# Attention in groups of three key blocks: another order for the evacuation, for GpSimd's preparation, for the adds and for a weight decode

## The chip, the cores and the metric

The kernel runs on one core of a Trainium2 chip. Five engines work side by side, each on a list of its own in the order in which the program issues it: TensorE (PE, with its weight loads PEld), VectorE (DVE), ScalarE (ACT), GpSimd (POOL) and SyncE (SP), which here only issues DMA transfers. An instruction that waits holds up everything behind it on its engine. The metric is the time of one execution on the device in microseconds.

## The reference, cut to what matters

Attention over pooled queries, then two mixture and gating stages on its output. The change touches the attention alone; 16 heads are worked on as 8 pairs.

```python
q_pool = q.reshape(B, H, S // 2, 2, D).mean(axis=3)            # B 2, H 8, S 1152, D 64
scores = scale * np.matmul(q_pool, k.transpose(0, 1, 3, 2))
scores = scores - np.max(scores, axis=-1, keepdims=True)
attn = np.exp(scores)
attn = attn / (np.sum(attn, axis=-1, keepdims=True) + 1e-09)
x = np.matmul(attn, v)
...
x = _moe_ref(x, ...)       # routing to 8 experts by argmax
x = _moe2_ref(x, w_in, w_out)
```

## The kernel before, in words

**Steps.** A pair of heads `p` has 9 blocks of 128 keys; one block is a step `t`, and `g = 9p + t` counts steps through all 8 pairs. In each step the loop at L655 to L679 issues, in this order: `scores(p, t)` (eight products and three exponentials into a tile `Pt`); the functions of slot 0; the early ("pre") maximum products; the functions of slot 1; in every third step the products of three finished blocks with v (`pv`, 24 products); in step 0 the evacuation `evac_x` of the finished pair; in step 6 `max_rows`; then `psums`, the row sums of the three blocks by products with a small matrix; in step 0 `evac_s`; the functions of slot 2; the late ("post") maximum products; the functions of slot 3. `at_step(p, t, f, slot=k)` puts a function into a slot. The last pair works in groups of two blocks.

**Exact products.** Queries and keys are split into a rounded part and a rest. `qhi`, `khi` (ScalarE) write the rounded parts `QS` and `At`, `qlo` (VectorE) and `klo` (GpSimd, tile `Bt`) the rests, `qcopy` (GpSimd) copies a half of `QS` to `qb`. They work one or two pairs ahead: in the loop `n = p + 1` and `m = p + 2`. `load_k`, `load_q`, `load_v` and `load_raw` issue the transfers; a key tile `kd` has two buffers, so `load_k` waits until `khi`, `klo` and `kdiff` of an earlier one are done.

**Maxima.** The row maximum of a unit (128 queries of a head; 9 units in a pair) comes from three products over 384 keys (`max_chunk`, c = 0, 1, 2), c = 1 against the key difference `KD` (tile `kx`, made by `kdiff` on GpSimd). ScalarE applies Relu to c = 1 and writes it to SBUF, VectorE reduces c = 0 and merges c = 2 with that. `step_chunks` deals them out to the steps, one pair ahead or two. Three PSUM buffers `mx` serve them. `max_cols` and `max_rows` turn the maxima into two rows of `qb`.

**Sums.** For three blocks VectorE adds the first two (`add_tile`, tile `st`), and `psums` takes that sum and the third. `psums` writes the same PSUM banks that `evac_x` reads.

**Weights.** The weights of the last stage arrive as 64-bit numbers and are decoded in the shadow of the attention: 23 tiles here. `raw_ahead` loads up to two tiles ahead, `decode_step` does one half of a tile (VectorE), `decode_abs` the absolute values (ScalarE) that the second half needs. `decode` calls `decode_abs` itself where it has not run yet.

## Time and profile of the kernel before

| what | us |
|---|---|
| median of three runs | 717.72 (716.46 to 718.08) |
| the profiled execution | 715.45 |
| its span, first to last instruction | 713.3 |
| first scores of pair 0 | 21.87 |
| first row sums of pair 1, step 0 | 67.88 |
| the same of pair 7 | 281.86 |
| last row sums | 314.74 |

Over the span TensorE is busy 90%, VectorE 69%, ScalarE 55%, GpSimd 30%. The attention is the stretch from 21.87 to about 317 us. In the rows below a line number is that of the kernel before; L91, L94, L97 and L100 are helpers that many functions share, so there the names of the tiles tell what an instruction is: `wd<-pv` on ACT is `evac_x`, `sm<-pv` `evac_s`, `wd<-mx` Relu, `dm` the absolute values and the decode, `st<-pt` the add, `kx<-kd` `kdiff`, `Bt<-kd,at` `klo`, `qb<-qs` `qcopy`, `qs<-tq` `qhi` on ACT and `qlo` on DVE. L324 are the products with v, L349 those of the row sums, L307 to L316 the scores. A bracket tells how long the engine had been idle before the instruction, and what ended that.

### The profile page before, as it was taken

To read this page: it belongs to the slowest core of one execution; us is meant where nothing else is said; L and a number is where in the kernel's file an instruction comes from. 1 tells how busy PE (TensorE), PEld (TensorE's weight loads), DVE (VectorE), ACT (ScalarE), POOL (GpSimd) and SP (SyncE) were. 2 spreads that over 40 slices of the span, in tenths; PEclk is the share of its full clock that TensorE was granted. 3 is DMA by queue.
4 is the path that set the end of the run, shared out by engine and by line. 5 is a ranking of instruction groups with operands and counts; after the bars stand their busy time and mean duration, and the time that the engine had idled before them with its cause. 6 is when DMAs were issued, how large, how long until landed. Compare 5 with 4: busy or idle time off the path is not lost. (4 is left out here: it accounts for less than half of the span.)

```text
span 713.3 us, 11655 instructions
## 1 busy us (share of the span) xinstructions
PE 644.0 (90%) x4319; PEld 510.2 (72%) x4319; DVE 490.4 (69%) x1010; ACT 391.9 (55%) x811; POOL 211.1 (30%) x195
## 2 busy tenths in 40 slices
PE   4798999997979999876998999997899999999997
PEld 3566766765757676545886886966788899999895
DVE  5667867674746764775745697611999977897875
ACT  7766776765655665522425546532666554555543
POOL 7443342423313120003503323410322232232322
PEclk9989999999998999998998999999999999999999
DMA  6674535352533112307839978682000020001001
GB/s 225 224 213 122 158 106 141 107 164 79 150 91 96 50 64 78 119 19 235 332 137 330 356 257 309 238 292 74 0 1 0 1 91 1 0 1 45 1 0 44
DMA packets 26641, 88.33 MB, mean 124 GB/s; under 512 B 2886, under 2 KB 7631, under 8 KB 22482
## 3 DMA queue, kind: packets, MB, share of 16 engines
q1 hardware_dynamic: 21264, 73.23, 29.3%
q0 software_dynamic: 3568, 8.79, 5.3%
q10 hardware_dynamic: 1746, 5.51, 2.2%
q8 instruction: 35, 0.57, 0.3%
q14 instruction: 28, 0.23, 0.1%
HBM read 79.65 MB, written 8.39 MB: 123 GB/s over the span
## 5 line engine op out<-in xcount | busy, mean ns | idle before, releaser
L91 ACT ACTIVATE pt<-sc 128x320 f32<-128x320 f32 (+1 forms) x216 | 96.5, 489 | 24.7 <-PE sc L309 23.3
L100 POOL TENSOR_SCALAR u<-u 128x384 f32<-128x384 f32 x48 | 60.2, 1255 | 152.1 <-ACT u L91 122.9
L324 PE MATMUL pv<-pt,vt 128*64 128x288 f32 x576 | 78.9, 424 | 0.0
L94 POOL TENSOR_TENSOR Bt<-kd,at 64x576 fp32r<-64x576 f32 x32 | 54.7, 1729 | 64.3 <-PE sc L310 59.1
L915 PE MATMUL zps<-yh,wh 128*128 128x384 f32 x188 | 64.3, 342 | 1.7 <-DVE n L97 1.7
L324 PEld LDWEIGHTS pv<-pt,vt 128*64 128x64 f32 x576 | 40.5, 142 | 32.9 <-issue 10.8
L917 PE MATMUL zps<-yl,wh 128*128 128x384 f32 x188 | 63.3, 337 | 0.0
L916 PE MATMUL zps<-yh,wd 128*128 128x384 f32 x180 | 61.0, 339 | 0.0
L1355 PE MATMUL ops<-wh,gl 128*128 128x512 f32 x144 | 57.7, 403 | 3.0 <-DVE gl L94 2.5
L103 DVE TENSOR_REDUCE Mp<-mx 128x1 f32<-128x384 f32 x72 | 39.9, 554 | 29.6 <-PE mx L230 29.4
L1355 PE MATMUL ops<-wh,gh 128*128 128x512 f32 x144 | 56.8, 395 | 0.2 <-ACT gh L91 0.2
L1355 PE MATMUL ops<-wd,gh 128*128 128x512 f32 x135 | 53.1, 394 | 0.0
L230 PE MATMUL mx<-at,qs 128*128 128x384 f32 x120 | 38.1, 388 | 12.4 <-DVE qs L94 7.7
L91 ACT ACTIVATE l<-n,two 128x384 f32<-128x384 f32 x48 | 29.5, 615 | 25.0 <-DVE n L97 25.0
L94 DVE TENSOR_TENSOR st<-pt 128x1152 f32<-128x1152 f32 x25 | 39.1, 1566 | 5.2 <-ACT pt L91 5.1
L91 ACT ACTIVATE wd<-mx 128x384 f32<-128x384 f32 x63 | 29.1, 498 | 22.7 <-PE mx L230 11.7
L91 ACT ACTIVATE u<-zps 128x384 f32<-128x384 f32 x48 | 23.2, 483 | 33.1 <-PE zps L917 30.0
L97 DVE SCALAR_TENSOR_TENSOR l<-n,r 128x384 f32<-128x384 f32 x48 | 26.6, 554 | 19.4 <-ACT r L91 19.4
L915 PEld LDWEIGHTS zps<-yh,wh 128*128 128x128 f32 x188 | 35.6, 189 | 3.6 <-ACT r L91 2.0
L244 DVE CUSTOM_DVE_ANT_0 wd<-mx,wd 128x384 f32<-128x384 f32 x63 | 34.5, 549 | 4.3 <-PE mx L230 2.9
L1355 PEld LDWEIGHTS ops<-wh,gl 128*128 128x128 f32 x144 | 27.0, 188 | 14.0 <-DVE gl L94 7.1
L91 ACT ACTIVATE gh<-n 128x384 fp32r<-128x384 f32 x48 | 24.8, 517 | 20.6 <-DVE n L97 20.4
(297 smaller groups left out, 1702.0 us busy)
## 6 DMA issues: line engine op xcount, KB each, us to landing
wt<-in_w SPq DMA_DIRECT2D x32, 1024.0 KB, 5.6
kd<-in_kt SPq DMA_DIRECT2D x16, 576.0 KB, 3.8
wraw<-in_wio SPq DMA_DIRECT2D x12, 512.0 KB, 4.0
wd<-in_wio SPq DMA_DIRECT2D x11, 512.0 KB, 4.5
vt<-in_v SPq DMA_DIRECT2D x8, 576.0 KB, 5.1
wraw<-in_wio ACTq DMA_DIRECT2D x9, 512.0 KB, 6.1
tq<-in_qt SPq DMA_DIRECT2D x12, 288.0 KB, 5.9
tq<-in_qt POOLq DMA_DIRECT2D x12, 288.0 KB, 5.2
```

Of the source, the lines that this page charges most:

```text
L91: A.activation(out=out, in_=in_, func=func, **kw)
L94: eng.tensor_tensor(out=out, in0=a, in1=b, op=op)
L97: V.scalar_tensor_tensor(out=out, in0=a, scalar=s, in1=b, op0=op0, op1=op1)
L100: eng.tensor_scalar(out=out, in0=a, scalar1=s1, scalar2=s2, op0=op0, op1=op1)
L103: V.tensor_reduce(out=out, in_=in_, axis=AX.X, op=op)
L230: mm(ps, lhsT=QS[p, h][:, j * P:(j + 1) * P], rhs=keys(h), start=True, stop=True)
L244: V.tensor_tensor_reduce(out=r_, in0=ps, in1=r_, scale=1.0, scalar=-3.0e38, op0=ALU.add, op1=ALU.max, accum_out=Mp[p % 2][:, h, j, 1:2])
L324: mm(pvt[p][64 * h:64 * h + 64, f, :HQ], lhsT=vt[p][:, t, h, :], rhs=Pt[p, t][:, h, f * HQ:(f + 1) * HQ], start=t == 0, stop=t == KT - 1, ...
L915: mm(out_, lhsT=a, rhs=c, start=first, stop=False)
L916: mm(out_, lhsT=b_, rhs=c, start=False, stop=False)
L917: mm(out_, lhsT=a, rhs=d, start=False, stop=last_)
L1355: mm(opt[b_, j], lhsT=(g_, g_, gl_)[i], rhs=(wo, wl_, wo)[i], start=f == 0 and i == 0, stop=f == NF - 1 and i == 2)
```

## The change

- `psums` is issued ahead of `evac_x`, in step 0 of each pair and at the end.
- `add_tile` runs in the step of its group (0, 3 and 6), behind the pre products, in place of the step before (2, 5, 8).
- GpSimd's `klo`, `qcopy` and `kdiff` of the pairs ahead go to slot 3 of steps 0, 3 and 6, and each lot but pair 0's starts with `after(n, u)`, a copy of one column on GpSimd that reads the maximum of unit `u`, c = 0, and so waits for it.
- `qhi`, `khi`, `qlo` of pair m move between steps; `khi(m, 1)` goes to step 0 of the next pair, so `at` needs 5 buffers and not 6. `load_k` and `load_q` go one step later.
- `decode_abs` ahead of need runs only for loads that are at least three steps old; `raw_ahead` runs behind the halves; pairs 1 to 6 take 5 halves each (before 5 and 4 in turn), the last pair correspondingly fewer.
- In pair 0 the products c = 1 run one step ahead, those of the first two units ahead of its first scores in place of two filler products. `x_tr`, `x_out` move behind the post products.

```diff
--- before.py
+++ after.py
@@ -175,7 +175,7 @@
         SP.dma_start(out=vt[p], in_=v[p])
 
     DEC_M = 32
-    DEC_A, DEC_L = 23, [2, 2, 1, 2, 2, 1, 2, 2, 1]
+    DEC_A, DEC_L = 23, [2, 1, 2, 1, 2, 1, 2, 1, 2]
     tqt = {}
 
     def qsum(p, h):
@@ -194,8 +194,13 @@
     def qmix(p, h):
         act(QM[p % 2][:, 192 * h:192 * h + 64], QS[p, h][:, 4 * P:].bitcast(F32))
 
+    def qb_(p, h):
+        if (p, h) not in QB:
+            QB[p, h] = ap.tile([P, SQ], F32R, name="qb", bufs=NBL)
+        return QB[p, h]
+
     def qcopy(p, h):
-        QB[p, h] = ap.tile([P, SQ], F32R, name="qb", bufs=NBL)
+        qb_(p, h)
         if p:
             G.tensor_copy(QB[p, h][:64], QS[p, h][:64].bitcast(F32))
         else:
@@ -203,7 +208,7 @@
 
     def khi(p, h, c):
         if c == 0:
-            At[p, h] = ap.tile([P, S], F32R, name="at", bufs=NB)
+            At[p, h] = ap.tile([P, S], F32R, name="at", bufs=NB - 1)
         cs_ = slice(c * SQ, (c + 1) * SQ)
         act(At[p, h][:, cs_], kd[p, h][:, cs_])
 
@@ -256,13 +261,12 @@
 
     units = [(h, j) for h in range(2) for j in range(4)] + [(0, 4)]
     chunks = ahead(units)
-    FIRST = [[0, 1], [2], [3], [4, 5], [6, 7], [8]]
+    FIRST = [[0, 1], [2], [3], [4, 5], [6, 7], [8], []]
 
     def step_chunks(p, t):
 
         if p == 0 and t < 6:
-            us = FIRST[t]
-            return [(1, *units[u], c) for c in (1, 0) for u in us], [(1, *units[u], 2) for u in us]
+            return [(1, *units[u], c) for u in FIRST[t] for c in (0, 2)], [(1, *units[u], 1) for u in FIRST[t + 1]]
         n, u = (p + 1, t + 3) if t < 6 else (p + 2, t - 6)
         if n >= NPAIR:
             return [], []
@@ -289,7 +293,7 @@
         ps1 = mxp.tile([P, 512], F32, name="mx")
         T.transpose(ps1[:34, :P], mt[:, 4, :], ident)
         for h in range(2):
-            qb = QB[p, h]
+            qb = qb_(p, h)
             act(qb[64:66, :512], ps0[32 * h:32 * h + 2, :])
             act(qb[64:66, 512:], ps1[:2, 64 * h:64 * h + 64])
 
@@ -334,9 +338,11 @@
         g = 9 * p + t
         return [divmod(i, KT) for i in range(g - 3, g)] if t % 3 == 0 and g else []
 
-    def add_tile(p, t):
-        St[p] = ap.tile([P, 2, SQ], F32, name="st", bufs=1)
-        tt(V, St[p], Pt[p, t - 2], Pt[p, t - 1], ALU.add)
+    def add_tile(tiles):
+        p = tiles[0][0]
+        if len(tiles) > 1:
+            St[p] = ap.tile([P, 2, SQ], F32, name="st", bufs=1)
+            tt(V, St[p], Pt[tiles[0]], Pt[tiles[1]], ALU.add)
 
     def psums(tiles):
         p = tiles[0][0]
@@ -467,9 +473,10 @@
         (SP if pool is ap else A).dma_start(out=wraw[i].rearrange("p a b -> p (a b)"), in_=wio[f, :, 512 * c:512 * (c + 1)].bitcast(I32))
 
     def decode_abs(pool, i=None):
-        if i is None:
+        early = i is None
+        if early:
             i = dec[0] + (dec[0] in dmt)
-        if i not in dmt and i in wraw:
+        if i not in dmt and i in wraw and now[0] - since.get(i, 0) >= (3 if early else 0):
             m = dmt[i] = pool.tile([P, 512], F32, name="dm", bufs=2)
             act(m, wraw[i][:, :, 1].bitcast(F32), AF.Abs)
 
@@ -504,66 +511,68 @@
     at_step(-1, 7, lambda: qhi(1, 0))
     at_step(-1, 8, lambda: max_cols(0), lambda: (qlo(1, 0), qmix(1, 0)))
     at_step(0, 0, lambda: (khi(1, 0, 1), klo(1, 0, 0), klo(1, 0, 1), load_k(2, 0), load_q(2, 0)))
-    at_step(0, 1, lambda: (qsum(1, 1), qhi(1, 1), khi(1, 1, 0), khi(1, 1, 1), kdiff(1, 1), qlo(1, 1), qmix(1, 1)), slot=1)
-    at_step(0, 2, lambda: (klo(1, 1, 0), klo(1, 1, 1), qcopy(1, 0), load_k(2, 1), load_q(2, 1)), slot=1)
-    at_step(0, 3, lambda: (qhi(2, 0), khi(2, 0, 0)), slot=1)
-    at_step(0, 4, lambda: (khi(2, 0, 1), kdiff(2, 0), qlo(2, 0)), slot=1)
-    at_step(0, 5, lambda: qcopy(1, 1), slot=1)
-    at_step(0, 6, lambda: (qhi(2, 1), khi(2, 1, 0), khi(2, 1, 1), kdiff(2, 1)), slot=1)
-    at_step(0, 7, lambda: qlo(2, 1), slot=1)
+    at_step(0, 1, lambda: (qsum(1, 1), qhi(1, 1), khi(1, 1, 0), kdiff(1, 1), qlo(1, 1)), slot=1)
+    at_step(0, 2, lambda: khi(1, 1, 1))
+    at_step(0, 3, lambda: qmix(1, 1), slot=1)
+    at_step(0, 2, lambda: (klo(1, 1, 0), klo(1, 1, 1), load_k(2, 1), load_q(2, 1)), slot=1)
+    at_step(0, 3, lambda: (qhi(2, 0), qlo(2, 0)), slot=1)
+    at_step(0, 4, lambda: (kdiff(2, 0), qcopy(1, 0)), slot=1)
+    at_step(0, 6, lambda: (khi(2, 0, 0), khi(2, 0, 1), qhi(2, 1), qlo(2, 1)), slot=1)
+    at_step(0, 6, lambda: (qcopy(1, 1), kdiff(2, 1)), slot=3)
     at_step(-1, 8, lambda: load_v(0))
+    wait_ = ap.tile([P, 1], F32, name="wait")
+
+    def after(n, u):
+        if n < NPAIR:
+            h, j = units[u]
+            G.tensor_copy(wait_, Mp[n % 2][:, h, j, 0:1])
+
+    def piece(k):
+        return [lambda: decode_step(ap, DEC_A)] * k + [lambda: raw_ahead(ap, DEC_A)]
+
+    def abs_():
+        return lambda: decode_abs(ap)
+
     for p in range(NPAIR):
         n, m = p + 1, p + 2
         if n < NPAIR:
             at_step(p, 4, lambda n=n: load_v(n), slot=1)
             at_step(p, 6, lambda n=n: max_cols(n))
             if p:
-                at_step(p, 0, lambda n=n: (klo(n, 0, 0), klo(n, 0, 1)))
-                at_step(p, 1, lambda n=n: (klo(n, 1, 0), klo(n, 1, 1)))
-                at_step(p, 3, lambda n=n: qcopy(n, 0), slot=2)
-                at_step(p, 5, lambda n=n: qcopy(n, 1), slot=1)
+                at_step(p, 0, lambda n=n: (after(n, 3), klo(n, 0, 0), klo(n, 0, 1), klo(n, 1, 0)), slot=3)
+                at_step(p, 3, lambda n=n: (after(n, 6), klo(n, 1, 1), qcopy(n, 0)), slot=3)
+                at_step(p, 6, lambda n=n: (after(n + 1, 0), qcopy(n, 1)), slot=3)
         if m < NPAIR:
             if p:
-                at_step(p, 0, lambda m=m: (qhi(m, 0), qhi(m, 1)), slot=1)
-                at_step(p, 1, lambda m=m: load_k(m, 0), slot=1)
-                at_step(p, 3, lambda m=m: (kdiff(m, 0), khi(m, 0, 0), khi(m, 0, 1), qlo(m, 0), qlo(m, 1), load_k(m, 1)), slot=1)
-                at_step(p, 6, lambda m=m: (khi(m, 1, 0), khi(m, 1, 1), kdiff(m, 1)), slot=1)
+                at_step(p, 2, lambda m=m: load_k(m, 0), slot=1)
+                at_step(p, 3, lambda m=m: (qhi(m, 0), qhi(m, 1), qlo(m, 0)), slot=1)
+                at_step(p, 3, lambda m=m: kdiff(m, 0), slot=3)
+                at_step(p, 4, lambda m=m: load_k(m, 1), slot=1)
+                at_step(p, 6, lambda m=m: (khi(m, 0, 0), khi(m, 0, 1), qlo(m, 1)), slot=1)
+                at_step(p, 6, lambda m=m: kdiff(m, 1), slot=3)
+            at_step(p + 1, 0, lambda m=m: (khi(m, 1, 0), khi(m, 1, 1)), slot=1)
             at_step(p + 1, 0, lambda m=m: (qmix(m, 0), qmix(m, 1)), slot=3)
         if p + 3 < NPAIR:
-            at_step(p, 6, lambda p=p: (load_q(p + 3, 0), load_q(p + 3, 1)), slot=2)
+            at_step(p, 7, lambda p=p: (load_q(p + 3, 0), load_q(p + 3, 1)), slot=1)
         if p:
             at_step(p, 4 if p == last else 3, lambda p=p: sum_log(p - 1), slot=1)
             at_step(p, 6, lambda p=p: (sum_tr(p - 1), sum_rec(p - 1)), slot=1)
-            at_step(p, 6, lambda p=p: [(x_tr(p - 1, i), x_out(p - 1, i)) for i in range(2)], slot=2)
+            at_step(p, 6, lambda p=p: [(x_tr(p - 1, i), x_out(p - 1, i)) for i in range(2)], slot=3)
             if p < last:
                 at_step(p, 8, lambda p=p: x_put(p - 1), slot=1)
-        if p < last:
-            for t in (2, 5, 8):
-                at_step(p, t, lambda p=p, t=t: add_tile(p, t))
-        else:
-            for t in (2, 4, 6, 8):
-                at_step(p, t, lambda p=p, t=t: add_tile(p, t))
-
-        def piece(k):
-            return [lambda: (raw_ahead(ap, DEC_A), decode_step(ap, DEC_A))] * k
-
-        def ahead_(k=1):
-            return [lambda: (raw_ahead(ap, DEC_A), decode_abs(ap))]
-
         if p == last:
             for t in range(9):
-                at_step(p, t, *piece(DEC_L[t]), *ahead_(), slot=1)
+                at_step(p, t, *piece(DEC_L[t]), slot=1)
+                at_step(p, t, abs_(), slot=3)
         else:
             if p == 0:
                 at_step(0, 0, lambda: raw_ahead(ap, DEC_A), slot=3)
             else:
-                at_step(p, 0, *piece(2), *ahead_(), slot=1)
-            at_step(p, 3, *piece(2), *ahead_(), slot=1)
-            if p == 0:
-                at_step(p, 6, *piece(2), slot=1)
-            elif p % 2:
-                at_step(p, 6, *piece(1), slot=1)
-            at_step(p, 6, *ahead_(), slot=2)
+                at_step(p, 0, *piece(2), slot=1)
+                at_step(p, 3, *piece(2), slot=1)
+            at_step(p, 3, abs_(), slot=2)
+            at_step(p, 6, *piece(2 if p == 0 else 1), slot=1)
+            at_step(p, 6, abs_(), slot=2)
 
     A.preload_act_table_set("natural_log_exp_and_others")
     load_q(0, 0)
@@ -612,11 +621,12 @@
     G.tensor_copy(tri, cc("tri"))
     G.tensor_copy(iota16, iota)
 
-    dec = [0, 0, 0]
+    dec, now, since = [0, 0, 0], [0], {}
 
     def raw_ahead(pool, end):
         while dec[2] < min(dec[0] + 2, end):
             load_raw(dec[2], pool)
+            since[dec[2]] = now[0]
             dec[2] += 1
 
     def decode_step(pool, end):
@@ -646,7 +656,8 @@
             assert not chunks
             warm(6)
             max_rows(0)
-            warm(2)
+            for u in FIRST[0]:
+                max_chunk(1, *units[u], 1)
 
     def run(g, slot):
         for f in sched.get((g, slot), ()):
@@ -654,24 +665,26 @@
 
     for g in range(9 * NPAIR):
         p, t = divmod(g, 9)
+        now[0] = g
         scores(p, t)
         run(g, 0)
         pre, post = step_chunks(p, t)
         for c_ in pre:
             max_chunk(*c_)
+        tiles = groups(p, t)
+        if tiles:
+            add_tile(tiles)
         run(g, 1)
-        tiles = groups(p, t)
         for i in tiles:
             for f in range(2):
                 pv(*i, f)
         end = tiles and tiles[-1][1] == KT - 1
-        if end:
-            evac_x(p - 1)
         if t == 6 and p < last:
             max_rows(p + 1)
         if tiles:
             psums(tiles)
         if end:
+            evac_x(p - 1)
             evac_s(p - 1)
         run(g, 2)
         for c_ in post:
@@ -679,8 +692,8 @@
         run(g, 3)
     for f in range(2):
         pv(last, KT - 1, f)
+    psums([(last, KT - 1)])
     evac_x(last)
-    psums([(last, KT - 1)])
     evac_s(last)
     sum_log(last)
     sum_tr(last)
```

## Rows read from the trace of the kernel before

**Rows 1.** The seven stretches between pairs: us, busy (x) of five engines, PEclk, DMA, GB/s

```profile
67.88:101.45 33.57, 32.09 (x287) 23.62 (x287) 24.85 (x56) 24.17 (x54) 13.02 (x11) 1.00 0.51 150
101.45:136.67 35.22, 32.59 (x287) 23.60 (x287) 24.49 (x56) 23.72 (x53) 13.00 (x11) 1.00 0.44 122
136.67:174.37 37.70, 32.58 (x287) 23.61 (x287) 25.86 (x59) 24.37 (x54) 13.01 (x11) 1.00 0.44 128
174.37:212.91 38.54, 33.90 (x286) 24.77 (x286) 23.45 (x56) 23.34 (x53) 11.86 (x11) 0.95 0.39 112
212.91:250.09 37.18, 34.95 (x287) 25.96 (x287) 24.24 (x58) 22.46 (x51) 10.11 (x9) 0.92 0.23 71
250.09:281.86 31.77, 30.35 (x277) 22.18 (x277) 18.76 (x47) 18.19 (x42) 4.25 (x5) 1.00 0.24 75
281.86:314.74 32.88, 28.08 (x245) 18.12 (x245) 25.42 (x50) 14.82 (x32) 0.24 (x1) 0.95 0.23 79
```

**Rows 2.** TensorE's waits, 60 to 360 us: total us, times, longest

```profile
PE pv L349 <- ACT wd L91: 11.4, 8, 3.3
```

**Rows 3.** Timeline at the start of pair 5: start us, us, engine line; then its clock

```profile
211.66 0.66 ACT L91 ACTIVATE dm<-wd 128x512 f32<-128x512 f32 x1 [2.76 <-DMA wd<-in_wio]
...
212.91 1.29 PE L349 MATMUL pv<-st,e 128*32 128x160 f32 x16 [3.32 <-ACT wd L91]
...
215.00:219.00 4.00, 4.00 (x20) 3.79 (x15) 1.79 (x5) 2.42 (x7) 3.12 (x4) 0.50 0.47 146
```

**Rows 4.** Timeline of ScalarE and TensorE at the start of pair 2

```profile
100.75 0.65 ACT L91 ACTIVATE wd<-pv 128x576 f32<-128x576 f32 x1 [0.23 <-PE pv L324]
...
101.45 0.75 PE L349 MATMUL pv<-st,e 128*32 128x160 f32 x16 [0.81 <-ACT wd L91]
...
102.81 0.43 ACT L91 ACTIVATE sm<-pv 64x320 f32<-64x320 f32 x1 [1.41 <-PE pv L349]
103.50 0.49 ACT L91 ACTIVATE wd<-mx 128x384 f32<-128x384 f32 x1 [0.26 <-PE mx L230]
...
104.18 1.24 ACT L91 ACTIVATE pt<-sc 128x320 f32<-128x320 f32 x3
```

**Rows 5.** Timeline of step 5 of pair 2: GpSimd, VectorE, TensorE

```profile
116.33 2.06 POOL L94 TENSOR_TENSOR Bt<-kd,at 64x576 fp32r<-64x576 f32 x1
...
116.52 3.11 DVE L94 TENSOR_TENSOR st<-pt 128x1152 f32<-128x1152 f32 x1
...
120.15 0.44 PE L230 MATMUL mx<-kx,qs 128*128 128x384 f32 x1 [1.12 <-DVE Mp L103]
```

**Rows 6.** Timeline of GpSimd: two subtractions, a key difference, two query copies

```profile
101.65 2.84 POOL L94 TENSOR_TENSOR Bt<-kd,at 64x576 fp32r<-64x576 f32 x2
104.45 1.00 POOL L94 TENSOR_TENSOR kx<-kd 128x384 fp32r<-128x384 f32 x1
...
178.27 1.27 POOL L200 CAST qb<-qs 64x576 fp32r<-64x576 f32 x2
```

**Rows 7.** VectorE: timeline in pair 2; tile view of the adds (ns min/median/max)

```profile
103.79 0.56 DVE L103 TENSOR_REDUCE Mp<-mx 128x1 f32<-128x384 f32 x1
...
108.25 1.43 DVE L94 TENSOR_TENSOR qs<-tq,qs 64x576 fp32r<-64x576 f32 x2
...
113.78 0.56 DVE L103 TENSOR_REDUCE Mp<-mx 128x1 f32<-128x384 f32 x1 [1.26 <-PE mx L230]
...
L94 DVE TENSOR_TENSOR st<-pt x25: 1351/1355/3112, 31.4 to 310.6; 128x1152 f32<-128x1152 f32 x25
```

**Rows 8.** Timeline of the last pair, steps 5 and 6: ScalarE, TensorE

```profile
298.65 0.66 ACT L91 ACTIVATE dm<-wd 128x512 f32<-128x512 f32 x1 [1.65 <-DMA wd<-in_wio]
...
299.69 0.41 PE L307 MATMUL sc<-qs,at 128*128 128x320 f32 x1 [1.60 <-ACT pt L91]
```

**Rows 9.** Pair 0: TensorE's timeline at step 3, and a stretch (columns as rows 1)

```profile
34.20 0.62 PE L230 MATMUL mx<-kx,qs 128*128 128x384 f32 x2 [0.73 <-POOL kx L94]
...
36.00:40.00 4.00, 3.75 (x15) 1.96 (x17) 2.40 (x6) 3.83 (x7) 1.45 (x2) 0.50 0.51 154
```

## Prediction

> **What bounds the kernel now.** I read the busy time by stretch first. Cut at the first row sums of each step 0, pairs 1 to 6 hold the same products, but for the maxima that pair 6 no longer has, and should last alike. They don't [rows 1]: pair 1 takes 33.57 us with TensorE busy for 32.09, pair 3 37.70 with 32.58. TensorE sets the pace, and what the slow pairs have more is idle time, and in pairs 4, 5 and 7 a granted clock of 0.92 to 0.95. So the question is what TensorE waits for.
>
> The view of waits names the largest: the row sums behind the evacuation of the products with v, 11.4 us in 8 times [rows 2]. The timeline shows two kinds. In a plain pair ScalarE evacuates at once, and TensorE, which could have gone on, stands 0.81 us [rows 4]. At the start of pair 5 ScalarE stood ahead of the evacuation in an absolute value whose weights had not landed; it waited 2.76 us for the transfer, so TensorE waited 3.32, and the four microseconds from 215 on were run at 0.50 of the clock, which is the lower of its two levels, 1.2 GHz [rows 3]. The same wait on a transfer costs the last pair 1.60 us at its exponentials [rows 8]. A third kind is short: in pair 2 VectorE's add took 3.11 us instead of 1.35, because a GpSimd subtraction ran from 116.33 to 118.39; the reduce behind it was late, and TensorE waited 1.12 us for its buffer [rows 5, 7].
>
> **The change part by part.** The sum is made against the profiled execution: 715.45 us, of which 713.3 are span and 2.15 lie around it. The median of the three runs is 717.72, so 2.27 are added at the end.
>
> *Row sums ahead of the evacuation.* It removes the 0.81 us of TensorE. Not all of that comes back. ScalarE now does the evacuation (0.65) behind the sums, where it had been waiting 1.41 for them anyway; `evac_s`, the Relu, two `qmix` and the exponentials of step 1 come behind. It had 0.26 idle ahead of the Relu [rows 4], so these exponentials start about 0.65 - 0.26 = 0.4 later after the sums, and in steps 1 and 2 TensorE follows the exponentials. Gain 0.81 - 0.4 = 0.4 us a pair; the bounds are 0 (TensorE falls back by all of the delay) and 0.81. VectorE's `evac_s` add and the maxima behind it also come 0.65 later. At the end of the attention evacuation, sums and `evac_s` only change places, which I cost at 0.
>
> *Absolute values of old loads.* By the order of issue a load of pairs 1 to 6 is at least three steps old when ScalarE takes it, also where `decode` takes it itself, and in the last pair two steps. A group of three steps is over 10 us, so the transfers have landed. This takes away the 3.3 us at the starts of pairs 4 and 5 (the first counted in the stretch of pair 3, the second in that of pair 4) with the low clock behind each. The count of halves stays; pairs 1 to 6 take three more in all, the last pair three fewer, beside TensorE's work.
>
> *GpSimd held.* What is queued behind the waiting copy on GpSimd are three `klo` in step 0, a `klo`, a `qcopy` and a `kdiff` in step 3, a `qcopy` and a `kdiff` in step 6 and the adds' transfers of `load_q`; who waits for that are the products with `kx`, the scores of the next pair, and SyncE, whose `load_k` needs the old key tile free, with the raw loads, `load_v`, `load_q` queued behind it. In microseconds after the sums of step 0: the maximum that releases the first lot was done at 103.79 + 0.56 - 101.45 = 2.9 [rows 4, 7], now 3.55. Three `klo` at 1.42 [rows 6] end at 7.8. VectorE comes to its add at about 6.5, meets them, and in the worst case starts at 7.8 and ends at 9.2; the sums want it at about 11, so that collision has cover. Behind it VectorE has one `qlo` and two halves. Its list of step 3 ran before from 108.25 to 113.78 - 1.26 = 112.52, so 4.27 with two `qlo` [rows 7]; without one it is 3.55 and ends at 12.75. The maximum that releases the next lot ran at 12.33 before and comes at 12.75 now, done at 13.3. `klo` 1.42, `qcopy` 0.64, `kdiff` 1.0 end at 16.4 [rows 6]. TensorE wanted `kx` in pair 2 at 120.15 - 1.12 - 101.45 = 17.6 [rows 4, 5]. That is a slack of 1.2 us: I cost it at 0, and if the cover is gone, see the rivals. The copy that waits has no row; the nearest are the copies of 0.64 [rows 6], the bounds 0 and 0.64, and I take about 0.15, since one column is far less than 576. The lock on steps 2, 5 and 8, and with it pair 2's 1.12, goes, since the add no longer stands ahead of a reduce that TensorE waits for.
>
> The Trainium skill, SBUF — State Buffer, section "SBUF: two separate sides", says that VectorE and GpSimd share a port pair as an exclusive lock, that a VectorE instruction with two SBUF inputs needs it against a GpSimd one that reads SBUF, and that the later comer blocks for the whole instruction. The 3.11 us agree. By that rule the add in step 3 cannot be hidden from the three `klo`, which speaks against this part; it is the second rival.
>
> *Smaller moves.* `x_tr` behind the post products lets ScalarE start on Relu earlier but waits itself for a buffer; I take 0 (bounds -0.3 and +0.3). The other moves change places among equal work on ScalarE.
>
> *The sum.* Pair 1 had no wait on a transfer and no late reduce: 33.57 - 0.4 = 33.2 us is the clean pair. Pairs 1 to 5 then give back 0.4, 2.0, 4.5, 5.3 and 4.0, together 16.2 [rows 1]. Pair 6 gives 0.4. The last pair was 32.88 at a clock of 0.95 [rows 1], so 0.05 x 32.88 = 1.6 of its work went to the clock; with the wait of 1.60 [rows 8], the 0.4 and one more such wait that could be up to 1.4 it is 3.6 to 5.0; as its steps may turn out bound by ScalarE I take 4. Pair 0: TensorE waits there 0.73 for `kx` at 34.20 and then runs four microseconds at 0.50 [rows 9]. The change asks for that same `kx` in step 2 instead of 3, and puts two Relu ahead of the first exponentials, so this start is not better and may be 1 worse; its later steps lose the late reduce and 0.4. I take -1 (bounds +1 and -3). Sum: 16.2 + 0.4 + 4 + 1 = 21.6. 715.45 - 21.6 = 693.9, with 2.27 added 696.1.
>
> **The rivals.**
>
> *More.* The busy time of a full-speed pair is 32.1 to 32.6 [rows 1]. If the exponentials don't hold TensorE back and pair 0 gains 3, another 5 to 7 come: about 690. For it speaks that 0.81 is pure waiting; against it that pair 1 kept 1.48 idle with only part of that at the evacuation.
>
> *The lock moves with the add.* If the add in step 3 waits out all three `klo` and the halves push the maxima back, each of pairs 1 to 6 pays what pair 2 paid over pair 1, 35.22 - 33.57 = 1.65 [rows 1]: 9.9 us, so 706. For it speaks that the meeting is certain; against it the 1.8 us of cover ahead of the sums, and that no add is left in steps 2, 5 and 8.
>
> *The change doesn't do what it says.* `decode` still takes absolute values by itself, and a raw load can sit on SyncE behind a `load_k`. If ScalarE still waits there, pair 3, 4, 5 and 7 keep 2.5, 5.3, 4.0 and 4: 15.8 back, so 712. Against it speaks the order of issue, by which each load has a group's time.
>
> *Slower.* The hold makes `kx` late. From the release by the maxima to the product in step 6 there is 1.2 us of slack; each microsecond more is a wait of TensorE, in pairs 1 to 5. In pair 4 a wait of 3.3 cost 38.54 - 33.2 = 5.3 with its clock [rows 1, 3], a factor of 1.6. The gain of 21.6 is eaten when each of five pairs loses 4.3, that is at a wait of 2.7, so from GpSimd being 3.9 us later than my timeline; at a wait of 4 it is 5 x 6.4 = 32, so 728. For it speaks that before `kdiff` ran right behind the evacuation, at 104.45 [rows 6], with 13 us to spare, and that one late reduce now moves everything on GpSimd; against it that the lot is only 3.1 us long.
>
> **How the numbers follow.** Forecast 0.53 (692 to 701 by its bounds), more 0.12, the lock 0.17, not as said 0.08, slower 0.08, and 0.02 for mixtures that cancel. The range takes in the first four: 689 to 713. Faster by over 0.2% (1.4 us, about what a measurement of this kernel can tell from no change): 0.53 + 0.12 + 0.17 + 0.08 less 0.02 = 0.88; within 0.03; slower 0.09.
>
> **What the profile after would show.** Right: row sums no longer wait for ScalarE; no wait of ScalarE on a transfer in the absolute values of pairs 1 to 6; pairs 1 to 5 of equal length near 33.2 and a clock of 1.00 from pair 1 on; the exponentials of step 1 start 3.1 us after the sums, against 2.73. Wrong: waits of TensorE on `kx` in step 6 with low clock behind, adds of 3 us in step 3 with the maxima late, or pairs 4, 5 and 7 still at a clock below 1.

## The result, and the profile after

The kernel after takes 694.53 us, the median of 4 runs (693.83 to 700.16), against 717.09 for the kernel before, 4 runs (712.35 to 718.08): 0.9715 of the time by the means of the runs, 95% interval 0.9648 to 0.9782. The forecast was 696.1 with a range of 689 to 713. The profiled execution took 693.83, with a span of 692.0; the sum of the prediction had put that execution at 693.9.

The busy time by stretch, cut at the first row sums of step 0 as in [rows 1], columns as there (us; busy time and count of TensorE, its weight load, VectorE, ScalarE, GpSimd; granted clock; DMA share; GB/s). The eighth line is the front of the last pair:

```profile
66.73:99.77 33.04, 32.42 (x288) 23.69 (x286) 23.32 (x57) 24.02 (x54) 12.30 (x14) 1.00 0.56 154
99.77:132.88 33.11, 32.48 (x288) 23.69 (x287) 24.20 (x60) 23.47 (x53) 12.27 (x14) 1.00 0.49 138
132.88:165.99 33.11, 32.46 (x289) 23.68 (x287) 23.62 (x59) 24.03 (x54) 12.26 (x14) 1.00 0.49 138
165.99:199.09 33.10, 32.45 (x289) 23.67 (x287) 24.21 (x60) 23.45 (x53) 12.27 (x14) 1.00 0.50 138
199.09:232.30 33.21, 32.58 (x289) 23.80 (x288) 23.98 (x59) 24.04 (x54) 10.58 (x12) 1.00 0.35 110
232.30:263.67 31.37, 30.69 (x279) 22.19 (x277) 21.71 (x51) 18.12 (x42) 8.46 (x9) 1.00 0.23 80
263.67:293.66 29.99, 27.83 (x247) 17.78 (x245) 23.18 (x46) 15.51 (x33) 0.24 (x1) 0.94 0.24 83
263.67:272.49 8.82, 7.56 (x66) 4.66 (x65) 5.76 (x10) 4.92 (x10) 0.24 (x1) 0.84 0.20 63
```

Pairs 1 to 5 are now equal, 33.0 to 33.2 us, where they were 33.6 to 38.5, and their clock is 1.00 throughout. The last pair is the only stretch here with a clock below 1.

TensorE's waits from 20 to 320 us (total us, times, longest), two lines of the attention:

```profile
PE mx L235 <- POOL kx L94: 2.9, 1, 2.9
...
PE sc L311 <- ACT pt L91: 1.2, 1, 1.2
```

The wait of [rows 2] has no line any more. The largest that is left is one of 2.9 in pair 0; the 1.2 is in the last pair. The start of pair 2, which [rows 4, 7] show for before, in the timeline (start us, us, engine line; in brackets the idle time ahead and what ended it): ScalarE, then TensorE, GpSimd and VectorE:

```profile
101.19 0.65 ACT L91 ACTIVATE wd<-pv 128x576 f32<-128x576 f32 x1 [2.06 <-PE pv L355]
...
103.01 1.24 ACT L91 ACTIVATE pt<-sc 128x320 f32<-128x320 f32 x3
...
99.77 0.75 PE L355 MATMUL pv<-st,e 128*32 128x160 f32 x16
...
117.52 0.53 PE L235 MATMUL mx<-kx,qs 128*128 128x384 f32 x2
...
103.54 0.18 POOL L528 COPY wait<-Mp 128x1 f32<-128x1 f32 x1 [1.39 <-DVE Mp L103]
103.69 5.30 POOL L94 TENSOR_TENSOR Bt<-kd,at 64x576 fp32r<-64x576 f32 x3
...
115.44 1.01 POOL L94 TENSOR_TENSOR kx<-kd 128x384 fp32r<-128x384 f32 x1
...
106.32 1.39 DVE L94 TENSOR_TENSOR st<-pt 128x1152 f32<-128x1152 f32 x1
109.14 0.76 DVE L94 TENSOR_TENSOR qs<-tq,qs 64x576 fp32r<-64x576 f32 x1 [1.43 <-POOL Bt L94]
```

The sums no longer wait; the exponentials of step 1 start 103.01 - 99.77 = 3.24 us after them (forecast 3.1). The key difference that step 6 needs ends at 116.45 and TensorE comes for it at 117.52: a slack of 1.07 (forecast 1.2). The tile view of the adds answers the last line of [rows 7] (ns min/median/max; the longest was 3112):

```profile
L94 DVE TENSOR_TENSOR st<-pt x25: 1349/1353/1394, 40.8 to 290.4; 128x1152 f32<-128x1152 f32 x25
```

### The profile page after: what moved, and what is told of

It reads as the page before. It is cut to its first block, busy times and chain, and to the rows that moved or that the text cites. A ratio compares the mean times of both kernels' runs of the same rounds, so it can differ in the third digit from the quotient of the medians.

```text
span 692.0 us, 11704 instructions
## 1 busy us (share of the span) xinstructions
PE 642.5 (93%) x4317; PEld 508.7 (74%) x4317; DVE 481.3 (70%) x1010; ACT 391.5 (57%) x811; POOL 211.4 (31%) x212
## 5 line engine op out<-in xcount | busy, mean ns | idle before, releaser
L94 POOL TENSOR_TENSOR Bt<-kd,at 64x576 fp32r<-64x576 f32 x32 | 51.8, 1647 | 6.8 <-ACT at L91 6.8
L91 ACT ACTIVATE wd<-mx 128x384 f32<-128x384 f32 x63 | 28.7, 496 | 23.6 <-PE mx L239 16.6
L94 DVE TENSOR_TENSOR st<-pt 128x1152 f32<-128x1152 f32 x25 | 34.0, 1360 | 4.2 <-ACT pt L91 4.2
```

What stands on the lines that cost most here:

```text
L91: A.activation(out=out, in_=in_, func=func, **kw)
L94: eng.tensor_tensor(out=out, in0=a, in1=b, op=op)
```

## The experiments

Whole times of one kernel spread over 3 to 10 us between executions. To judge by the profiled executions of kernels that share these parts, most of that lies in pair 0's first group, in the first group of the last pair and behind the attention. So the edits are compared by the lengths of pairs 1 to 6: between the kernel after and the three kernels that leave these pairs alone (those of the last part) they agree to 0.13 us. Every time is of a kernel's profiled execution unless a median is named; each ratio is to the kernel before, on the same chip.

### Undoing the order at the group's end

In the kernel after, the evacuation goes ahead of the sums again:

```diff
         end = tiles and tiles[-1][1] == KT - 1
+        if end:
+            evac_x(p - 1)
 ...
             psums(tiles)
         if end:
-            evac_x(p - 1)
             evac_s(p - 1)
```

> The changed kernel (694.5 us) with the evacuation put back ahead of the row sums in step 0 of each pair and at the end; all else as changed. My theory: TensorE waits 0.8 us again at eight places, but the exponentials of step 1 come 0.5 earlier after the sums, so the net loss is 0.3 to 0.4 a pair, 2.5 to 3 in all: 697 to 697.5. Rival, all of the wait is lost: 8 x 0.81 = 6.5, so 701. Rival, the order is worth nothing: 694.5.

Pairs 1 to 6: 33.50, 33.46, 33.46, 33.49, 33.58 and 31.74, that is 0.35 to 0.46 more each. Median 695.81, ratio 0.9725 (0.9676 to 0.9774). The view of waits of this kernel, 60 to 330 us, has the old line back:

```profile
PE pv L355 <- ACT wd L91: 6.4, 8, 0.8
```

0.8 us of waiting costs 0.4 of a pair: the half that the prediction had taken off for later exponentials is really lost.

### That order alone, in the kernel before

The same swap made in the kernel before, and nothing else (the lines of the diff above, in the other direction).

> The kernel before (717 us) with one part alone: row sums ahead of the evacuation. My theory: 0.3 to 0.4 us in each plain pair; where ScalarE stands on a transfer (two starts of pairs) TensorE now goes on with sums, maxima and scores and meets it 2.9 us later at the exponentials, so most of 3.3 is filled and the low clock behind it goes: 2 x 4 more. About 706 to 709. Rival, the wait only moves to the exponentials: 714 to 716.

Median of 10 runs 716.47, ratio 0.9956 (0.9914 to 0.9998): by the whole time the swap alone is worth less than 1%, and the theory of 706 to 709 fell. The profiled execution is the slowest of the ten (719.78), so of its stretches only those without a wait on a transfer are compared: pairs 1, 2 and 6 are 0.5, 0.6 and 0.8 longer than in [rows 1], where 0.4 each was to be had. What took the gain there, in the view of waits from 60 to 330 us and in the timeline at the start of pair 3 (VectorE, GpSimd, TensorE) of this kernel:

```profile
PE mx L230 <- DVE Mp L103: 8.4, 12, 1.8
...
147.03 3.49 DVE L94 TENSOR_TENSOR st<-pt 128x1152 f32<-128x1152 f32 x1
...
147.08 1.01 POOL L94 TENSOR_TENSOR kx<-kd 128x384 fp32r<-128x384 f32 x1
148.04 1.27 POOL L200 CAST qb<-qs 64x576 fp32r<-64x576 f32 x2
...
151.04 0.44 PE L230 MATMUL mx<-kx,qs 128*128 128x384 f32 x1 [1.81 <-DVE Mp L103]
```

GpSimd's first work of a pair stands behind a copy of the evacuated tile, so with the evacuation later its two `klo` start 2.3 us after the sums (144.27), where they started 0.2 after [rows 4, 6]. The add then falls on the key difference and two query copies, lasts 3.49 instead of 1.35, and the maximum behind it is late. The waits on ScalarE have become waits on VectorE's maxima (in the kernel before 3.8 us in 3 times, here 8.4 in 12). The swap is worth something only together with the parts that move the add and GpSimd's work.

### Old loads alone, in the kernel before

```diff
-        if i not in dmt and i in wraw:
+        if i not in dmt and i in wraw and now[0] - since.get(i, 0) >= (3 if early else 0):
```

with the step number kept at each load, as in the change.

> The kernel before with one part alone: absolute values ahead of need only from loads at least three steps old. My theory: this is the largest part; the waits at two starts of pairs with the low clock behind them go, and those of step 3 in pairs 4 and 5 and of the last pair: 10 to 14 us, 703 to 707. Rival, decode's own call then stands at the same place and waits as long: 713 to 717.

Median 700.33, ratio 0.9756 (0.9697 to 0.9816). Stretches of pairs 2, 3, 4 and the last pair:

```profile
101.86:137.07 35.21, 32.57 (x286) 23.60 (x286) 24.48 (x56) 23.71 (x53) 13.00 (x11) 1.00 0.45 122
137.07:172.30 35.23, 32.60 (x286) 23.60 (x287) 25.83 (x59) 24.29 (x54) 13.00 (x11) 1.00 0.42 117
172.30:205.89 33.59, 32.12 (x286) 23.64 (x286) 24.08 (x56) 23.61 (x53) 13.04 (x11) 1.00 0.45 128
...
271.70:301.87 30.17, 26.16 (x245) 17.27 (x245) 25.25 (x50) 15.05 (x33) 0.23 (x1) 1.00 0.27 87
```

The clock is 1.00 in all of them, and in pairs 1 and 5 (33.59 and 34.06). Pairs 1 to 6 (the sixth 31.75) fall from 213.98 to 203.43, the last pair from 32.88 to 30.17: 13.3 us of the change's gain lie in this one condition. What stays are two pairs of 35.2, which is the length of pair 2 in [rows 1].

### Absolute values of any age, in the kernel after

The other direction: the condition on age is taken out of the kernel after, while the new places of the absolute values stay.

```diff
-        if ... and now[0] - since.get(i, 0) >= (3 if early else 0):
+        if ... and now[0] - since.get(i, 0) >= 0:
```

> The changed kernel with absolute values taken ahead of need from loads of any age. By the order of issue, pairs 2, 4 and 6 then take one in step 3 and one in step 6 from a load of the same step, and the last pair three more in steps 0, 2, 3 and 4. My theory: ScalarE waits about 4 us for each, TensorE loses about 1 in each of the six and some 3 in the last pair, with some low clock: 700 to 706. Rival, the waits are hidden since the evacuation no longer stands between them and TensorE: 694 to 696.

Pairs 1 to 6: 32.95, 33.00, 33.00, 33.00, 33.12, 31.30. Nothing is lost there. In the last pair the way from its first sums to those of step 8 takes 29.57 instead of 28.18. Median 699.09, ratio 0.9764 (0.9709 to 0.9819). The profiled execution is 7.5 us longer than that of the kernel after: 1.4 is the last pair, 4.1 pair 0's first group (sums at 49.12) and 2.6 lies behind the last sums, neither of which the edit reaches. In pairs 1 to 6 ScalarE's absolute values waited for a transfer twice, 1.26 us in pair 2 and 1.96 in pair 4, and neither pair is longer for it. The last pair has three such waits of 1.87 to 2.29; against the two kernels whose last pair ran without a low clock (26.55 and 26.59, see the last part) they cost it 3.0 and not 1.4. So in pairs 1 to 6 the new places (steps 3 and 6, behind the sums, with `raw_ahead` behind the halves) do without the age rule what that rule did in the kernel before: few loads are still under way there, and what is left to wait for is hidden. Undoing one of two covers shows nothing.

### Any age, and one absolute value in step 0 again

To tell place from age: as the last, and an absolute value goes back ahead of the evacuation in step 0.

```diff
-                at_step(p, 0, *piece(2), slot=1)
+                at_step(p, 0, *piece(2), abs_(), slot=1)
```

> The changed kernel with absolute values taken from loads of any age and, beside steps 3 and 6, also in slot 1 of step 0, where the kernel before had them: ahead of the evacuation, and from a load that the same step issues in pairs 2 to 6. e2, with any age alone, left pairs 1 to 6 at 33.0. My theory: the place and not the age alone makes the wait dear; ScalarE now stands before evacuation and exponentials of step 1, so pairs 2 to 6 lose 1 to 4 us each at their start: stretches of 34 to 37. Rival, the sums ahead of the evacuation cover it there too: 33.0 to 33.4.

One run, 713.6 us. Pairs 1 to 6: 33.02, 33.11, 41.43, 33.10, 41.95, 31.38. Two pairs lose 8.3 and 8.7, the others nothing, where the theory had small losses in all. Pair 3, in ScalarE's timeline and by stretch:

```profile
135.21 0.66 ACT L91 ACTIVATE dm<-wraw 128x512 f32<-128x512 f32 x1 [3.64 <-DMA wraw<-in_wio]
...
150.83 0.67 ACT L91 ACTIVATE dm<-wd 128x512 f32<-128x512 f32 x1 [5.22 <-DMA wd<-in_wio]
...
132.20:146.60 14.40, 12.10 (x96) 8.91 (x94) 6.99 (x15) 8.48 (x20) 4.55 (x5) 0.88 0.24 75
146.60:162.77 16.17, 14.14 (x103) 11.35 (x101) 9.61 (x29) 6.82 (x16) 3.12 (x4) 0.79 0.42 142
```

The wait ahead of the evacuation is back (135.21), and behind it comes a second, in step 3 (150.83): 3.64 and 5.22 us of ScalarE. The two groups run at a clock of 0.88 and 0.79 and take 14.40 and 16.17 us, where the kernel after takes 11.1 for each. In pairs 2 and 4 of this kernel step 3 waits too, 1.85 and 2.27 us, and they keep their 33.1. So the length of a wait counts: behind the sums about 2 us are free, and 5.22 go with 5.1 more in that group. The 3.64 ahead of the evacuation go with 3.3 more in theirs; no run has a wait of that length behind the sums, or one of 2 us ahead of the evacuation, so the share of the place alone is not shown. What is shown is that one absolute value back in step 0 brings both waits.

### No hold on GpSimd

```diff
-            G.tensor_copy(wait_, Mp[n % 2][:, h, j, 0:1])
+            pass
```

> The changed kernel without the copy that makes GpSimd wait for a maximum; the places of klo, qcopy and kdiff in its list stay. My theory: the hold hides behind slack and buys little; the lots start 1 to 5 us earlier and meet VectorE's add either way: 693.5 to 696. Rival, the hold keeps GpSimd off VectorE's two-input instructions at a moment that matters: about 1 to 1.65 us a pair lost without it, 700 to 704.

Pairs 1 to 6: 33.43, 33.59, 33.46, 33.60, 33.59, 31.36. The first five lose 0.35 to 0.50 us each, 2.1 together. Median 697.74, ratio 0.9759 (0.9708 to 0.9810). The timeline at the start of pair 3, VectorE and GpSimd:

```profile
140.32 2.56 DVE L94 TENSOR_TENSOR st<-pt 128x1152 f32<-128x1152 f32 x1
143.12 1.86 DVE L94 TENSOR_TENSOR qs<-tq,qs 64x576 fp32r<-64x576 f32 x1 [0.24 <-issue]
...
136.10 5.56 POOL L94 TENSOR_TENSOR Bt<-kd,at 64x576 fp32r<-64x576 f32 x4
141.62 1.78 POOL L205 CAST qb<-qs 64x576 fp32r<-64x576 f32 x1
```

Without the hold GpSimd runs on from 136.10 without a gap; the add and the query subtraction take 2.56 and 1.86 instead of 1.39 and 0.76. Four subtractions in 5.56 are 1.39 each, so the fourth began near 140.27, just ahead of the add, which waits it out. The hold is worth 0.4 us a pair: more than the nothing of the theory, less than the 1.65 of the rival.

### The adds in steps 2, 5 and 8 again

```diff
+        if t in ((2, 5, 8) if p < last else (2, 4, 6, 8)):
+            add_tile([(p, t - 2), (p, t - 1)])
         run(g, 0)
 ...
-        if tiles:
-            add_tile(tiles)
```

> The changed kernel with the adds back in steps 2, 5 and 8 (2, 4, 6, 8 in the last pair), ahead of the maxima of that step. My theory: in step 2 the add now meets the three held klo, waits up to 2.8 us, the reduce behind it is late and TensorE waits for its buffer as in pair 2 of the kernel before: 1.1 to 1.65 us in each of six pairs, 701 to 704. Rival, VectorE gets its turn between two klo without TensorE noticing: 694 to 696.

Pairs 1 to 6: 33.32, 33.40, 33.44, 33.43, 33.53, 31.47, so 0.1 to 0.3 more each, and not the 1.1 to 1.65 of the theory. Median 697.97, ratio 0.9727 to 0.9823 around 0.9775. VectorE at the start of pair 3:

```profile
140.88 1.46 DVE L94 TENSOR_TENSOR st<-pt 128x1152 f32<-128x1152 f32 x1
142.26 0.54 DVE L103 TENSOR_REDUCE Mp<-mx 128x1 f32<-128x384 f32 x1
```

GpSimd's three subtractions had begun at 139.70, and the add still took only 1.46. Only in pair 0 is the meeting dear: the add of step 2 there takes 5.24 (34.45), and TensorE waits 4.0 for the maximum behind it. In pairs 1 to 6 what differs is the order: the maximum behind the add starts 6.47 us after the sums of step 0 (135.79), in the kernel after 5.60.

### GpSimd made late

In the kernel after, GpSimd copies 128x500 floats, which nothing uses, twice or eight times ahead of the key difference in step 3:

```diff
-                at_step(p, 3, lambda m=m: kdiff(m, 0), slot=3)
+                at_step(p, 3, lambda m=m: (late(2), kdiff(m, 0)), slot=3)
```

> The changed kernel with two copies of 128x500 on GpSimd ahead of kdiff(m, 0) in step 3 of pairs 1 to 5; they compute nothing that is used. By the copy of 64x576, 0.66 us, they cost some 1.15 together. In the changed kernel kdiff ended 1.07 us before TensorE's product wanted it. My theory: the cover takes nearly all, a pair goes from 33.1 to 33.1 to 33.4. Rival, the hold has no slack in truth: each of five pairs loses 1.15 or more, 34.2.

> The same with eight copies, some 4.6 us: GpSimd then ends 3.5 us after the product wants the key difference. My theory (the slower rival of the prediction): TensorE waits 3.5 us in step 6 of five pairs and runs at the lower clock level behind it, 3.5 to 5.6 us a pair, a pair of 36.6 to 38.7, 712 to 722 in all. Rival, the products behind it are short of work anyway and the wait is made up: pairs of 33.1 to 34.5, under 702.

One run each. Two copies take 1.26 us, just over the slack of 1.07: 697.63 us, pairs 1 to 5 at 33.34 to 33.50, 0.3 more each. Eight copies take 6.74: 735.18 us, 2.5% over the kernel before (717.2). Of the second, TensorE's waits (60 to 330 us), GpSimd's copies and TensorE's product in pair 2, and the group of pair 1 with the wait:

```profile
PE mx L235 <- POOL kx L94: 27.4, 5, 5.5
...
124.68 6.74 POOL L529 COPY slk<-slk 128x500 f32<-128x500 f32 x8
...
132.42 1.01 PE L235 MATMUL mx<-kx,qs 128*128 128x384 f32 x2 [5.49 <-POOL kx L94]
...
78.70:98.16 19.46, 13.95 (x102) 9.88 (x100) 9.49 (x27) 6.69 (x15) 9.38 (x12) 0.82 0.34 119
```

6.74 less the slack of 1.07 is 5.67; the wait was 5.49. The five pairs together take 205.79 against 165.57, so 40.2 us for 27.4 of waiting: 1.47 for each microsecond, since the group with the wait has a mean clock of 0.82. The slower rival was a real mechanism of this kernel; the kernel after has 1.07 us between itself and it.

### The two waits that are left

Pair 0 and the last pair each keep one wait. In pair 0, GpSimd, TensorE, and a stretch of the kernel after:

```profile
33.61 1.13 POOL L167 DMA_DIRECT2D tq<-in_qt  x1 [5.16 <-PE mx L235]
34.44 1.34 POOL L94 TENSOR_TENSOR kx<-kd 128x384 fp32r<-128x384 f32 x1
...
35.84 0.62 PE L235 MATMUL mx<-kx,qs 128*128 128x384 f32 x2 [2.89 <-POOL kx L94]
...
40.00:44.00 4.00, 4.00 (x18) 1.94 (x18) 2.87 (x5) 2.00 (x4) 0.00 (x0) 0.50 0.97 300
```

GpSimd stands 5.16 us ahead of an accumulating transfer; the key difference is queued behind it, TensorE waits 2.89 for that and runs at 0.50 of the clock from 40 to 44. The bracket names TensorE, but what the transfer needs is its first half in place, to which it adds: in the kernel of the next edit the same transfer waits 4.32 for that half (first line of the next rows). So the transfer goes behind the key difference (`acc_q` is the accumulating half of `load_q`):

```diff
-    at_step(0, 0, lambda: (..., load_k(2, 0), load_q(2, 0)))
-    at_step(0, 1, lambda: (..., kdiff(1, 1), qlo(1, 1)), slot=1)
+    at_step(0, 0, lambda: (..., load_k(2, 0), load_q(2, 0, False)))
+    at_step(0, 1, lambda: (..., kdiff(1, 1), acc_q(2, 0), qlo(1, 1)), slot=1)
```

> The changed kernel with one move in pair 0: GpSimd issues the accumulating transfer of the third pair's queries behind the key difference kdiff(1, 1) and not ahead of it. In the changed kernel that transfer waits for its first half to land (idle until 33.61), the difference runs at 34.44 and TensorE waits 2.89 us for it at 35.84 with a clock of 0.50 from 40 to 44. My theory: the wait goes and the low clock with it, 3 to 5 us: 689.5 to 691.5. Rival, TensorE then waits for the next thing (VectorE's maxima or ScalarE): 693 to 694.5.

Median 690.85, ratio 0.9611 (0.9562 to 0.9661). The first sums come at 40.53 instead of 45.05. The transfer, the product and the stretch in this kernel:

```profile
32.99 1.13 POOL L160 DMA_DIRECT2D tq<-in_qt  x1 [4.32 <-DMA tq<-in_qt]
...
33.35 0.82 PE L239 MATMUL mx<-kx,qs 128*128 128x384 f32 x2 [1.00 <-ACT wd L91]
...
40.00:44.00 4.00, 3.98 (x51) 2.93 (x47) 1.09 (x2) 2.57 (x7) 0.62 (x1) 1.00 0.94 230
```

In the last pair, ScalarE and TensorE of the kernel after, and a stretch:

```profile
266.22 0.66 ACT L91 ACTIVATE dm<-wd 128x512 f32<-128x512 f32 x1
266.91 1.25 ACT L91 ACTIVATE pt<-sc 128x320 f32<-128x320 f32 x3
...
267.40 0.41 PE L311 MATMUL sc<-qs,at 128*128 128x320 f32 x1 [1.19 <-ACT pt L91]
...
270.00:274.00 4.00, 4.00 (x32) 2.05 (x29) 3.62 (x7) 0.44 (x1) 0.00 (x0) 0.63 0.28 91
```

This absolute value waits for no transfer. It simply lies between the evacuation and the exponentials, 0.66 us long, in a pair that has no maxima left to keep TensorE busy. So move it ahead of the evacuation, where ScalarE is idle (3.60 in the last pair):

```diff
-                at_step(p, t, abs_(), slot=3)
+                at_step(p, t, abs_(), slot=3 if t else 1)
```

> The changed kernel with the first absolute value of the last pair in slot 1 of step 0, ahead of the products with v, and not in slot 3 behind evac_s. In the changed kernel it stands ahead of the exponentials of step 1, TensorE waits 1.19 us for these at 267.40 and runs at 0.63 of the clock from 270 to 274. My theory: 0.6 to 0.7 of wait goes at least, with the clock 1.5 to 2.5: 692 to 693. Rival, the exponentials are bound by the evacuation, not by this: 694 to 694.5.

Median 692.54, ratio 0.9646 (0.9589 to 0.9703). From the first sums of the last pair to its sums of step 8 it takes 25.86 us instead of 28.18. The front of the last pair in this kernel, against 8.82 at 0.84 above, and then the same front in the kernel without the hold, which leaves the last pair as it is in the kernel after:

```profile
262.95:269.69 6.74, 6.17 (x67) 4.24 (x65) 4.05 (x7) 4.28 (x9) 0.24 (x1) 1.00 0.20 62
...
265.77:273.19 7.42, 6.16 (x67) 4.23 (x65) 4.42 (x7) 4.93 (x10) 0.24 (x1) 1.00 0.22 73
```

So not all of the 2.3 is the move's. That kernel and the one with eight copies have the same wait of 1.2 and no low clock behind it: the same way takes them 26.55 and 26.59, where the kernel after, the one with two copies and the one of the first edit take 28.14 to 28.18. 0.7 us is the move's in either case; the other 1.6 is a low clock that followed this wait in three of five executions, and did not come in the two kernels with the move.

Both edits together:

> The changed kernel with both moves: in pair 0 the accumulating transfer behind the key difference, in the last pair the first absolute value ahead of the products with v. My theory: the two lie in different stretches (about 4 us in the first group of pair 0, 2.3 in the first group of the last pair by their traces), so they add: 688 to 689, against 717 to 719 for the kernel before. Rival, a start earlier by 4 us finds a transfer not landed and gives some back: 690 to 692.

Median of 6 runs 687.9 (685.65 to 691.22), ratio 0.9595 (0.9557 to 0.9634): faster than the kernel before, and its interval lies below that of the kernel after. By the first sums the first edit gives 2.6 here (41.67, against 44.30 in the kernel with the second edit alone) and gave 4.5 by itself.

## Why the prediction was right

Of the 21.62 us between the two profiled executions (715.45 to 693.83), 21.08 lie ahead of the last sums (314.74 to 293.66); the rest of the span changed by 0.22 and what lies around it by 0.32. The forecast for these parts was 21.6, 0 and 0. The main mechanisms were right; that the sum met this execution to 0.1 us is luck, since its parts missed by up to 1.1 and cancel, and those at the two ends of the attention differ between executions by more than that. That the median came 1.6 under the forecast is the offset: it was taken as 2.27 over the profiled execution, and was 0.70.

**Pairs 1 to 5.** The clean pair was put at 33.2 and measured 33.04 to 33.21. The five gave 0.53, 2.11, 4.59, 5.44 and 3.97, together 16.6, where 0.4, 2.0, 4.5, 5.3 and 4.0 were forecast; pair 6 gave 0.40 against 0.4. The method, one undisturbed pair less one measured wait and the rest brought to its length, needed no price for the low clock, since the pairs of [rows 1] already held it. Of the 17.0 that pairs 1 to 6 gave, the age rule alone gives 10.6 in the kernel before; undoing the order, the hold or the place of the adds in the kernel after takes 2.3, 2.1 and 1.6, each by itself.

**Sums ahead of the evacuation.** 0.4 forecast, 0.35 to 0.46 measured when undone. Right, with a condition that the prediction didn't name: alone in the kernel before, the swap makes the plain pairs longer, for the add then meets GpSimd.

**Old loads.** Right in size: the age rule alone gives 13.3, where the third rival had counted 15.8 for it, and no absolute value of pairs 1 to 6 waits for a transfer. But the prediction put it all on age. In the kernel after, pairs 1 to 6 stay clean without the age rule; it is worth 3.0 in the last pair.

**GpSimd held.** Slack 1.2 forecast, 1.07 measured; the waiting copy 0.15 forecast, 0.18 measured; cost 0 forecast, and it is a gain of 0.4 a pair. The lock of [rows 5] is gone, as forecast: no add takes over 1394 ns. The meeting in step 3 went otherwise than the worst case. The add at 106.32 took 1.39 in the middle of three subtractions; GpSimd paid, with 5.30 us for three that alone take 1.42 each, and VectorE's next subtraction, which waited 1.43 us. The tile view of these three (ns min/median/max):

```profile
L94 POOL TENSOR_TENSOR Bt<-kd,at x3: 1404/1427/2526, 103.7 to 106.5; 64x576 fp32r<-64x576 f32 x3
```

The second ends near 103.69 + 1.40 + 1.43 = 106.52, 0.2 us after the add began, and the third, behind the add, takes 2.53. The Trainium skill, SBUF — State Buffer, section "SBUF: two separate sides", has the later comer blocked for the whole instruction. The traces agree that one excludes the other. So the add does not wait for all three: between two of GpSimd's instructions VectorE can get in. That is why the second rival didn't come in pairs 1 to 6, here or with the adds in their old steps; in pair 0 VectorE can wait out all three (next paragraph).

**Pair 0.** -1 forecast, -1.15 measured, by two misses that cancel. The first group came 2.84 later (42.21 to 45.05) with bounds of +1: the step that failed is "this start is not better and may be 1 worse". It saw that `kx` is asked for earlier, but not what is queued ahead of it on GpSimd, the accumulating transfer; putting that behind gives 4.5 back, or 2.6 with the second edit in both. This group also differs between executions: 44.3 to 49.1 in kernels with the pair 0 of the kernel after, 42.2 to 47.1 in kernels with that of the kernel before. So the 2.84 from one execution of each is rough; the wait for `kx`, 0.73 before, is the firmer sign: 1.9 to 2.9 in all the kernels with the new pair 0 but one. The two groups after it gave 1.41 and 2.58 where the prediction reckoned with little more than 2. What makes the longest of these groups (49.1, in the kernel with absolute values of any age) stands in its VectorE timeline:

```profile
33.28 5.30 DVE L94 TENSOR_TENSOR qs<-tq,qs 64x576 fp32r<-64x576 f32 x1 [0.75 <-ACT qs L91]
```

The same subtraction takes 0.76 in the kernel with the second edit alone (44.3). Here it waits out GpSimd's key difference and two subtractions, which end at 37.96, and TensorE waits 6.0 for it. In the kernel of 47.1 (the order alone, in the kernel before) it is the add that meets them, 5.81 long, and TensorE waits 4.4. So the lock that the prediction feared for step 3 is met in pair 0, in some executions, with the old order there as with the new.

**The last pair.** 4 forecast with 3.6 as the lower end, 2.89 measured. The term of the old wait of 1.60 was right [rows 8]. What was missed is that its absolute values still stand ahead of the exponentials: an old load needs no wait, but its 0.66 us still come first, and in this execution a low clock followed. In the two kernels with the same last pair and no low clock it takes 28.35 and 28.39, a gain of 4.5, within the 3.6 to 5.0 of the forecast. So the term is short by a clock that comes and goes, and moving that absolute value gives 0.7 to 2.3.

**The rivals.** The lock moving with the add: the meeting happened, the price didn't. Not as said: absent. Slower by a late `kx`: not reached, by 1.07 us, and its factor of 1.6 per microsecond of wait measured 1.47. That the two lie close is in part chance: the 5.3 of pair 4 also held the low clock behind the wait at its own start and a second wait of ScalarE on a transfer (3.86 us in step 3), which the prediction put down to one wait of 3.3. More: not for the reason given (pairs 1 to 5 don't go below 32.9 in any kernel run here), though 688 was to be had at the two ends of the attention.

**What stays open.** Where the 0.1 to 0.3 us of the early adds are lost was followed only to the later maximum. What decides in which executions VectorE meets GpSimd in pair 0 was not tried. It is not known either why the same wait in the last pair is followed by a low clock in some executions only. No run put GpSimd's work back into its old steps, so what the new places are worth without the hold and the adds is not shown.

## What to carry to other kernels

Cut a repeated loop at the same instruction, take the one repeat that has no disturbance, and price a change by what brings the others to it; then look separately at the first and the last repeat, where other work is queued and nothing fills the waits. On an engine that runs in order, an instruction that may wait for a transfer belongs behind what the critical engine needs next, and where it stands counts beside how old its load is. A part that gains little alone, and one whose removal costs little, can both be needed: try each in the old kernel and in the new. Before a gain is put down to an edit, look in the other runs for the same stretch unchanged: here one of two effects came and went by itself.

## What the runs showed that was not expected

VectorE's add of 1152 elements began in the midst of three GpSimd subtractions issued back to back and took 1.39 and 1.46 us, while against a key difference and two copies it took 3.49, and in pair 0 it could wait for over 4 us. What decides who gets in was not settled. A copy of one column on GpSimd costs 0.18 us, and that is the whole price of a hold. Eight copies of 128x500 took 6.74 us where two took 1.26. The tile view of those in pair 2 (ns min/median/max) shows that it is not the copies:

```profile
L529 POOL COPY slk<-slk x8: 599/600/1693, 124.7 to 130.8; 128x500 f32<-128x500 f32 x8
```

Six of the eight take 0.60, as in the run of two. One, from 127.3, takes 1.69 while VectorE's add runs (127.22 to 128.56), and one, from 129.1, takes 1.01 beside VectorE's query subtraction: the same meeting as in step 3, and GpSimd pays again.
